# Attention's P V in a fused attention and mixture-of-experts kernel: fp32 operands in one product for three products of fp16 halves

## The chip, the cores and the metric

One Trainium2 chip (trn2), one of its cores. The metric is device time in microseconds of one execution of the whole kernel, taken as the median of several runs. The engines are named as in the profile: PE (TensorE matmuls), PEld (TensorE weight loads), DVE (VectorE), ACT (ScalarE), POOL (GpSimd), SP (the queue that issues most DMAs).

## What is computed

Attention over keys and values that are averaged in groups of 8, then a mixture-of-experts layer in which each token goes to its best expert. Batch 8, 8 heads, 576 tokens, head size 64; 72 pooled keys per head; 8 experts.

```python
k_p = k.reshape(B, H, Sp, pool, D).mean(axis=3)      # 576 -> 72 rows
v_p = v.reshape(B, H, Sp, pool, D).mean(axis=3)
scores = scale * np.matmul(q, k_p.transpose(0, 1, 3, 2))
attn = np.exp(scores - np.max(scores, axis=-1, keepdims=True))
attn = attn / (np.sum(attn, axis=-1, keepdims=True) + 1e-09)
x = np.matmul(attn, v_p)                             # tokens x (8 heads * 64)
logits = x @ w_gate
expert_idx = np.argmax(logits, axis=1)
gate_w = softmax(logits)[best]
y = relu(x @ w1[expert_idx]) @ w2[expert_idx]
out = gate_w * y
```

## The kernel before

**Units.** The 4608 tokens are handled in 36 units of 128 tokens (`units`, L447 to L456). A batch has 576 tokens, so four whole units and a rest of 64; the rests of two batches share one unit (its `r` is None), so two batches make nine units. The loop over units (L1029) writes the instructions of all engines in their final order; there is no scheduler. In it, work of neighbouring units is interleaved: while unit i has its P V, the scores of units i+3 or so are formed.

**A unit's steps.** `g_qt` turns the queries on PE (L471) and ACT copies them out (L476). `g_s` forms scores: two matmuls of 128x144 in fp32 for each call (L498; L492 in a unit of two rests), two calls per unit. `g_min` takes the row minima of the negated scores on DVE (L508), `g_exp` the exponentials on ACT (L515), written as P to a buffer `both`. `u_pt` turns P on PE (five transposes, L522) into the PSUM tile `pp`, and ACT copies it to SBUF (L527). `u_pv` multiplies by V into the PSUM tile `po`. `u_nrm` divides by the row sums on DVE: L589, a reciprocal L591 and a product L593 that writes the token rows. There is one `pp` and one `po`, so a unit's transposes wait until the copies of the last one have been read, and its P V waits for the last one's L593.

**P V in halves.** The eight heads' 72 keys lie one after the other, cut in five chunks of 128 rows (`HS`, `SLOTS`), so a chunk holds pieces of two or three heads. V is laid out as `VB[b % 3]`: for each chunk and each of up to three heads (its slots) the 64 columns of V, 8 gate columns and a column of ones, 73 in all, set to zero in the rows of other heads by a mask. All of it is held twice in fp16: half 0 is V rounded, half 1 the rest. P too: L527 writes `ph` (fp16 of 256 P), and L533 on DVE forms the rest, `pl` (256 P minus ph). `u_pv` then takes three passes, ph with both halves of V, pl with the first one:

```python
for x, y in ((0, 0), (0, 1), (1, 0)):
    a = (ph, pl)[x]
```

Each pass has six matmuls, two each of 146, 219 and 73 columns, 18 for a unit (L559), 36 where two batches share the unit (L554, 64 output rows each).

**Preparing V of a batch** (`prep`, L837, and the hand-written hooks for batch 1). POOL sums groups of eight rows (`pool_k`, `pool_v`: L326, L328, L329). `v_pe` and `v_act` turn V; `v_high` writes its fp16 half on ACT (L397); `u_pe` multiplies V by the gate weights (L416, L418) into a PSUM tile `pu`; `v_copy` on ACT copies the high half into `pu` too (L410). On DVE, `v_dve` forms the low half (L402), `cross` scales the gate columns by the mask (L427), `both_halves` writes their two halves (L430, L431). Then `masked` writes V times the mask into `VB`, once per half (L441, 128x960), in two units running; in each of these units PE multiplies the mask by an identity (L525) so that it lies in `pp` beside P.

**Order between DVE's pieces.** Small steps of the routing (`route`: best expert, rank, positions of six units at a time) and the three steps of `u_dve` wait in a list, `fillers`; `fill()` takes one at fixed places of a unit (L1053, L1055, within `u_nrm`), and the steps of V are put at the list's head (L435).

**After attention.** Rows are scattered by expert in DRAM (L708, POOL), and from L1199 on the experts' products follow on PE: `up` (L1009 to L1018) and `finish` (L1097), in a loop over blocks of 256 tokens. The first products of block 0 stand already in units 33 to 35 (`UPAT`).

Of the kernel before, what the change touches and what calls it, by code (L numbers as in the profile page):

```python
# [17 lines left out]
POOL = 8  # L18
SX = 2.0 ** 6
SW = 2.0 ** 5  # L20
SV = 4.0
SP = 256.0
# [10 lines left out]
def kernel(  # L33
# [116 lines left out]
    mks = consts.tile([128, 5, 3], F32, name="mks")  # L150
    nc.vector.tensor_scalar(mks, mk, SV, None, op0=OP.mult)
    mk16 = consts.tile([128, 5, 3], F16, name="mk16")
    z16 = consts.tile([128, 5, 3], F16, name="z16")
    nc.vector.memset(z16, 0.0)
    nc.vector.tensor_copy(mk16, mk)
# [46 lines left out]
    for e in range(E):  # L202
# [10 lines left out]
    VB = [loads.tile([128, 2, 5, 3, CS], F16, name=f"vb{i}") for i in range(3)]  # L213
# [5 lines left out]
               for x in (VB[2].rearrange("p y c s x -> p (y c s x)").bitcast(F32),  # L219
# [163 lines left out]
    def v_act(b):  # L383
# [8 lines left out]
        if b:  # L392
            v_high(b)

    def v_high(b):
        vc = KVS["vc", b] = work.tile([128, 2, 5, D], F16, name="vc", bufs=2)
        nc.scalar.activation(vc[:, 0, :, 0:D], KVS["vp", b], AF.Copy, scale=SV)  # L397

    def v_dve(b):
        vp, vc = KVS.pop(("vp", b)), KVS["vc", b]  # L400
        hi = vc[:, 0, :, 0:D] if b == 0 else five(KVS["pu", b], UX, D)
        nc.vector.scalar_tensor_tensor(vc[:, 1, :, 0:D], vp, SV, hi, op0=OP.mult, op1=OP.subtract)  # L402
# [17 lines left out]
    def u_dve(b):  # L420
        pm = KVS["pu", b]
        ut = pm[:, 0:UX].rearrange("p (c s e) -> p c s e", s=3, e=E)
        gh, gl = (VB[b % 3][:, s, :, :, D:D + E] for s in range(2))
# [94 lines left out]
    def u_pt(i):  # L518
# [7 lines left out]
        ph = work.tile([128, 640], F16, name="ph")  # L526
        nc.scalar.activation(ph, pp[:, 0:640], AF.Copy, scale=SP)  # L527
        PP_[i] = (pp, ph)

    def u_lo(i):  # L530
        pp, ph = PP_[i]
        pl = work.tile([128, 640], F16, name="pl", bufs=1)
        nc.vector.scalar_tensor_tensor(pl, pp[:, 0:640], SP, ph, op0=OP.mult, op1=OP.subtract)  # L533
        PP_[i] = (ph, pl)

    def u_pv(i):
        b, r = units[i]
        ph, pl = PP_.pop(i)
# [3 lines left out]
        for x, y in ((0, 0), (0, 1), (1, 0)):  # L542
            a = (ph, pl)[x]
# [829 lines left out]
```

## Times and profile before

| | us |
|---|---|
| median of 3 runs | 610.09 (606.8 to 613.31) |
| the profiled execution | 607.39 |
| its span, first to last instruction | 604.4 |
| mean granted clock of TensorE over the span | 0.986 of full |

The profile is of one execution. "Busy" of PE is the union of its matmul records, each of which also holds the time in which its last results drain, so a busy PE may still have room. A matmul in fp32 shows as two records and two weight loads, a transpose in fp32 and a matmul in fp16 as one. Times in the timeline are starts and lengths from the span's start; what the next instruction on PE starts after is the time that an instruction takes of the engine.

### The profile page before, as it was taken

Reading aid. Unit: us, or ns where it says so; the run is one execution under the profiler, and the core shown is the slowest. Engines: PE = TensorE matmul, PEld = TensorE weight load, DVE = VectorE, ACT = ScalarE, POOL = GpSimd, SP = SyncE. Lnnn points to the kernel's source line nnn. Section 1 sums busy time; section 2 is a strip of 40 time slices with the busy share of each in tenths; the row PEclk is TensorE's granted clock in tenths of the full one; section 3 lists DMA queues with packets and bytes.
Section 4 is the critical chain, followed back from the end, with each engine's and each line's share of the span. In section 5 each row is a group of like instructions: output and inputs, shape, how many; then the busy total and the mean of one; then the engine's idle time right before and its main releaser. Section 6 shows DMA issues by size and latency. Waiting matters only on the chain.

```text
span 604.4 us, 15782 instructions
## 1 busy us (share of the span) xinstructions
PE 568.9 (94%) x4727; PEld 421.1 (70%) x4728; DVE 309.9 (51%) x616; ACT 291.5 (48%) x648; POOL 270.5 (45%) x529
## 2 busy tenths in 40 slices
PE   7888999998899989979999999999999999999994
PEld 7687879887786746747676765767756767657762
DVE  5768888997887173206743872324513551123122
ACT  2777789889952262217643662224422642122222
POOL 5698898998976632120441331131421142201221
PEclk9999999999999989989999999999999999999997
DMA  8999898885586839832986789233242323421200
GB/s 231 303 291 281 279 310 276 269 254 196 139 312 194 237 98 387 282 90 39 337 287 165 223 253 318 77 95 80 73 109 44 93 61 90 109 62 32 65 35 15
DMA packets 96274, 107.14 MB, mean 177 GB/s; under 512 B 54446, under 2 KB 64686, under 8 KB 96240
## 3 DMA queue, kind: packets, MB, share of 16 engines
q1 hardware_dynamic: 89520, 85.42, 49.9%
q0 software_dynamic: 6720, 21.28, 9.3%
q8 instruction: 19, 0.31, 0.2%
q14 instruction: 15, 0.12, 0.1%
HBM read 72.99 MB, written 23.37 MB: 159 GB/s over the span
## 4 chain that ended last, share of the span: by engine, by line
PE 74%; DVE 9%; ACT 8%; POOL 3%; issue 2%; DMA 2%; SPq 0%; ACTq 0%; POOLq 0%; PEld 0%; DVEq 0%
PE po L1097 17%; PE pq L1097 15%; PE ps L1018 8%; PE pp L1018 4%; PE pq L1018 4%; PE ps L1009 3%; PE ps L1010 3%; PE ps L1011 3%; PE po L559 2%; ACT both L515 2%; PE ps L498 2%; PE pp L522 2%; PE pp L1009 2%; PE pp L1011 2%; PE pp L1010 2%
## 5 line engine op out<-in xcount | busy, mean ns | idle before, releaser
L1097 PEld LDWEIGHTS <-bd 128*128 128x128 f16 x936 | 91.4, 98 | 105.5
L1091 DVE SCALAR_TENSOR_TENSOR bd<-ps,bd 128x512 f16<-128x512 f32 (+1 forms) x44 | 27.6, 630 | 183.7 <-ACT bd L1088 183.6
L1258 POOL TENSOR_TENSOR spacer<-ql,iG 1x1 f32<-1x1 f32 x44 | 20.3, 462 | 196.2 <-ACT ql L1254 193.9
L515 ACT ACTIVATE both<-ps,nmx 128x72 f32<-128x72 f32 x288 | 68.5, 331 | 11.3 <-DVE nmx L508 10.3
L1088 ACT ACTIVATE bd<-ps 128x512 f16<-128x512 f32 (+1 forms) x44 | 24.0, 549 | 97.6 <-PE L1018 75.6
L1097 PE MATMUL po<-w,bd 128*128 128x512 f16 x264 | 58.9, 379 | 0.0
L1097 PE MATMUL po<-kv,bd 128*128 128x512 f16 x264 | 58.8, 379 | 0.0
L1018 PEld LDWEIGHTS <-qt 128*128 128x128 f16 x528 | 49.4, 101 | 12.5 <-issue 5.1
L1259 POOL DMA_INDIRECT out_dram<-ql,iG x44 | 46.2, 1051 | 21.4 <-issue 20.3
L1018 PEld LDWEIGHTS <-w 128*128 128x128 f16 x480 | 42.2, 100 | 9.9 <-ACT kv L116 2.6
L498 PE MATMUL ps<-bd,qT 128*128 128x144 f32 x256 | 45.6, 302 | 2.9 <-ACT both L515 0.9
L1097 PE MATMUL pq<-kv,bd 128*128 128x512 f16 x216 | 48.1, 379 | 0.0
L1097 PE MATMUL pq<-w,bd 128*128 128x512 f16 x192 | 42.9, 379 | 0.0
L1254 ACT ACTIVATE ql<-po,gB 128x512 f32<-128x512 f32 x22 | 15.0, 683 | 57.0 <-PE L1018 35.0
L708 POOL DMA_INDIRECT x_by_expert<-both,rpos x36 | 35.5, 987 | 14.1 <-issue 5.5
L498 PEld LDWEIGHTS ps<-bd,qT 128*128 128x128 f32 x256 | 34.8, 190 | 4.6 <-ACT both L515 1.4
L1018 PE MATMUL ps<-kv,qt 128*128 128x256 f16 (+1 forms) x264 | 32.9, 269 | 4.4 <-issue 4.0
L918 DVE TENSOR_TENSOR bd<-vb,bd 128x1024 f16<-128x1024 f32 x22 | 27.0, 1226 | 17.3 <-issue 7.3
L1254 ACT ACTIVATE ql<-pq,gB 128x512 f32<-128x512 f32 x22 | 15.0, 681 | 42.7 <-PE pq L1097 41.0
L533 DVE SCALAR_TENSOR_TENSOR pl<-pp,ph 128x640 f16<-128x640 f32 x36 | 29.5, 821 | 11.7 <-ACT ph L527 11.5
L326 POOL TENSOR_TENSOR st<-kv 128x1280 f32<-128x1280 f32 x12 | 34.9, 2905 | 0.0
L559 PE MATMUL po<-vb,ph 128*128 128x146 f16 (+2 forms) x384 | 30.4, 227 | 3.6 <-ACT ph L527 2.5
(259 smaller groups left out, 1296.6 us busy)
## 6 DMA issues: line engine op xcount, KB each, us to landing
both<-in_moe_w_dram SPq DMA_DIRECT2D x6, 2048.0 KB, 11.6
st<-in_moe_w_dram SPq DMA_DIRECT2D x6, 2048.0 KB, 14.3
vb<-x_by_expert SPq DMA_DIRECT2D x16, 578.0 KB, 5.8
st<-in_moe_w_dram SPq DMA_DIRECT2D x8, 1024.0 KB, 7.6
kv<-in_k_dram SPq DMA_DIRECT2D x6, 1024.0 KB, 8.2
kv<-in_v_dram SPq DMA_DIRECT2D x6, 1024.0 KB, 10.6
qt<-in_q_dram SPq DMA_DIRECT2D x6, 1024.0 KB, 11.8
kv<-in_k_dram SPq DMA_DIRECT2D x4, 512.0 KB, 4.8
```

The source lines that it names most:

```text
L326: nc.gpsimd.tensor_tensor(t1, src[:, :, 0:4 * D], src[:, :, 4 * D:], op=OP.add)
L498: nc.tensor.matmul(ps[:, x * 2 * KP:(x + 1) * 2 * KP], t[:, h, :], BD[b % 3][:, :, h, :], start=True, stop=True)
L515: nc.scalar.activation(p[:, h * KP:(h + 1) * KP], ps[:, x * KP:(x + 1) * KP], AF.Exp, bias=nmx[:, x:x + 1], scale=-1.0)
L559: nc.tensor.matmul(po[:, half, cols], a[:, c * 128:(c + 1) * 128], VB[b % 3][:, y, c, sl, 0:CW], start=st, stop=False, skip_group_check=True)
L708: st = nc.gpsimd.indirect_dma_start(out=xs, out_offset=bass.IndirectOffsetOnAxis(ap=Z["pos"][:, u:u + 1], axis=0), in_=X[:, u, :], in_offs ...
L1009: nc.tensor.matmul(dst, wh, xT[:, d, 0:n], start=(d == 0), stop=False)
L1010: nc.tensor.matmul(dst, wh, xT[:, DC + d, 0:n], start=False, stop=False)
L1011: nc.tensor.matmul(dst, wl, xT[:, d, 0:n], start=False, stop=(d == DC - 1))
L1018: nc.tensor.matmul(dst, W1[s][z][:, d, c], xT[:, x, 0:n], start=(z == 0 and x == 0), stop=(z == 1 and d == DC - 1))
L1097: nc.tensor.matmul(y, hT[x][:, f, 128 * j:128 * j + 128], W2[s][z][:, f, :], start=(half == x == z == f == 0), stop=(half == z == 1 and f ...
L1254: nc.scalar.activation(ys[j], pY[j], AF.Copy, scale=gB[:, j:j + 1])
L1259: st = nc.gpsimd.indirect_dma_start(out=out, out_offset=bass.IndirectOffsetOnAxis(ap=iG[:, j:j + 1], axis=0), in_=ys[j], in_offset=None, b ...
```

## The change

P and V stay in fp32. `u_pt` copies P once, unscaled, as fp32 (`pt`); `u_lo` and with it the low half of P are gone. `VB` has one fp32 copy in place of two fp16 ones, of the same size in bytes. `masked` runs once per batch and reads the pooled V itself, so `v_high`, `v_copy` and `v_dve` are gone. The gate columns are written by one product with the mask. `u_pv` has one pass of six matmuls in fp32. The scales of P and V (256 and 4) leave `u_nrm`. The mask is put beside P in one unit per batch where it was two.

```diff
-    VB = [loads.tile([128, 2, 5, 3, CS], F16, name=f"vb{i}") for i in range(3)]
+    VB = [loads.tile([128, 5, 3, CS], F32, name=f"vb{i}") for i in range(3)]
...
     def blank(i):
-        nc.gpsimd.memset(VB[i][:, 1, :, :, 72:73], 0.0)
-        nc.gpsimd.tensor_tensor(VB[i][:, 0, :, :, 72:73], mk16[:, :, :, None], z16[:, :, :, None], op=OP.add)
+        nc.gpsimd.tensor_tensor(VB[i][:, :, :, 72:73], mk[:, :, :, None], z15[:, :, :, None], op=OP.add)
...
-        if b:
-            v_high(b)
-
-    def v_high(b):
...
-    def v_dve(b):
...
-    def v_copy(b):
-        nc.scalar.activation(five(KVS["pu", b], UX, D), KVS["vc", b][:, 0, :, 0:D], AF.Copy)
...
         def cross():
-            KVS.pop(("pu", b))
-            nc.vector.tensor_tensor(ut, ut, mks[:, :, :, None].to_broadcast([128, 5, 3, E]), op=OP.mult)
-
-        def both_halves():
-            nc.vector.tensor_scalar(gh, ut, 1.0, None, op0=OP.mult)
-            nc.vector.tensor_tensor(gl, ut, gh, op=OP.subtract)
-            KVS["whole", b] = True
-
-        first = [lambda: v_dve(b)] * (b > 0) + [cross, both_halves]
-        fillers[0:0] = [(-1, False, f) for f in first]
-
-    def masked(b, s):
-        assert b == 0 or KVS["whole", b]
-        vc = KVS["vc", b] if s == 0 else KVS.pop(("vc", b))
+            nc.vector.tensor_tensor(VB[b % 3][:, :, :, D:D + E], ut, mk[:, :, :, None].to_broadcast([128, 5, 3, E]),
+                                    op=OP.mult)
+
+        fillers[0:0] = [(-1, False, cross)]
+
+    def masked(b):
         m = five(KVS["pp"], MK, 3) if b else KVS["m0"]
-        nc.vector.tensor_tensor(VB[b % 3][:, s, :, :, 0:D], vc[:, s, :, None, :].to_broadcast([128, 5, 3, D]),
+        nc.vector.tensor_tensor(VB[b % 3][:, :, :, 0:D], KVS.pop(("vp", b))[:, :, None, :].to_broadcast([128, 5, 3, D]),
                                 m[:, :, :, None].to_broadcast([128, 5, 3, D]), op=OP.mult)
...
-        ph = work.tile([128, 640], F16, name="ph")
-        nc.scalar.activation(ph, pp[:, 0:640], AF.Copy, scale=SP)
-        PP_[i] = (pp, ph)
-
-    def u_lo(i):
-        pp, ph = PP_[i]
-        pl = work.tile([128, 640], F16, name="pl", bufs=1)
-        nc.vector.scalar_tensor_tensor(pl, pp[:, 0:640], SP, ph, op0=OP.mult, op1=OP.subtract)
-        PP_[i] = (ph, pl)
+        pt = PP_[i] = work.tile([128, 640], F32, name="pt")
+        nc.scalar.activation(pt, pp[:, 0:640], AF.Copy)
...
-        for x, y in ((0, 0), (0, 1), (1, 0)):
...
+        for c in range(5):
+            h0, hend = HS[c] + SLOTS[c][0], HS[c] + SLOTS[c][1]
...
+                for s in range(2 if r is None else 1):
+                    m = slice(0, 128) if r is not None else slice(64 * s, 64 * s + 64)
+                    nc.tensor.matmul(po[m, half, cols], pt[:, c * 128 + m.start:c * 128 + m.stop],
+                                     VB[(b + s) % 3][:, c, sl, 0:CW], start=first.get(half, True), stop=False,
+                                     skip_group_check=True)
...
-    def put_masked(b, *at):
-        for s, i in enumerate(at):
-            mask_at.add(i)
-            put(i, "dve", masked, b, s)
+    def put_masked(b, at):
+        mask_at.add(at)
+        put(at, "dve", masked, b)
...
-        put(u[0], "act", v_copy, b)
...
-        u_lo(i)
```

On PE, between the scores of a unit and its P V, before the change (`ps` scores, `pq` turned queries and values, `po` the P V; one pass of three is shown):

```order
L498 MATMUL ps<-bd_159,qT 128x144 x2
L471 MATMUL pq<-ident,qt_154 128x128 x4
L375 MATMUL pq<-ident,vp 128x128 x2
L377 MATMUL pq<-ident,vp 64x128
L379 MATMUL pq<-ident,kp 64x64
L559 LDWEIGHTS ph
L559 MATMUL po<-vb_161,ph 128x146
L559 LDWEIGHTS ph
L559 MATMUL po<-vb_161,ph 128x219
L559 LDWEIGHTS ph
L559 MATMUL po<-vb_161,ph 128x73
```

And at the same step of a batch in the changed kernel, with the whole of its P V and what follows (a matmul in fp32 loads its weights itself and has one row):

```order
L467 MATMUL ps<-bd_154,qT 128x144 x2
L440 MATMUL pq<-ident,qt_151 128x128 x4
L368 MATMUL pq<-ident,vp 128x128 x2
L370 MATMUL pq<-ident,vp 64x128
L372 MATMUL pq<-ident,kp 64x64
L513 MATMUL po<-vb_159,pt 128x146
L513 MATMUL po<-vb_159,pt 128x219
L513 MATMUL po<-vb_159,pt 128x73
L513 MATMUL po<-vb_159,pt 128x146
L513 MATMUL po<-vb_159,pt 128x219
L513 MATMUL po<-vb_159,pt 128x73
L467 MATMUL ps<-bd_154,qT 128x144 x2
```

What stands ahead of P V is the same; the 18 matmuls on two tiles have become six on one.

On DVE, where the routing of six units meets the gate columns of a batch, before the change (`vc`, `vb` and `pq` of V and its gate columns, `ra`, `rm`, `roh` of the routing, `pl` the low half of P, `ri` and `both` of the division):

```order
L640 TENSOR_TENSOR pq<-pq,rm 128x48
L402 SCALAR_TENSOR_TENSOR vc<-vp,pq 128x320
L427 TENSOR_TENSOR pq<-pq,mks 128x120
L430 TENSOR_SCALAR vb_163<-pq 128x15x8
L431 TENSOR_TENSOR vb_163<-pq,vb_163 128x15x8
L589 TENSOR_SCALAR ri<-po 128x8
L646 TENSOR_TENSOR pq<-pq,down 128x48
L647 TENSOR_REDUCE rm_1937<-pq 128x6
L591 RECIPROCAL ri<-ri 128x8
L657 TENSOR_TENSOR roh<-pq,rm_1937 128x48
L593 TENSOR_TENSOR both<-po,ri 128x576
```

The same place in the changed kernel, up to the next unit's division:

```order
L595 TENSOR_TENSOR pq<-pq,rm 128x48
L403 TENSOR_TENSOR vb_159<-pq,mk 128x15x8
L544 TENSOR_SCALAR ri<-po 128x8
L601 TENSOR_TENSOR pq<-pq,down 128x48
L602 TENSOR_REDUCE rm_1596<-pq 128x6
L546 RECIPROCAL ri<-ri 128x8
L612 TENSOR_TENSOR roh<-pq,rm_1596 128x48
L548 TENSOR_TENSOR both<-po,ri 128x576
L477 TENSOR_REDUCE nmx<-ps 128x4 x2
L671 TENSOR_REDUCE rso<-roh 128x8
L544 TENSOR_SCALAR ri<-po 128x8
```

Four steps that read the tile of the gate columns have become one, and between the two minima of a unit there is no `pl`.

## Rows read from the trace of the kernel before

**Rows 1.** Busy us (and instructions) of each engine in four stretches of attention

```profile
core 0: us, PE busy (x) PEld busy (x) DVE busy (x) ACT busy (x) POOL busy (x), PEclk, DMA share, GB/s
39.34:58.09 18.75, 16.62 (x167) 14.44 (x167) 15.62 (x40) 14.13 (x48) 18.27 (x12) 1.00 1.07 290
58.09:122.88 64.79, 61.26 (x665) 55.91 (x663) 56.55 (x143) 56.36 (x184) 57.33 (x70) 1.00 0.89 284
122.88:163.22 40.34, 35.28 (x379) 31.70 (x378) 33.19 (x88) 36.76 (x109) 35.40 (x48) 1.00 0.61 196
163.22:180.87 17.65, 16.00 (x206) 13.83 (x205) 14.52 (x44) 11.02 (x31) 14.11 (x28) 1.00 0.87 280
```

**Rows 2.** The same for L533 alone, once per unit, in two stretches

```profile
58.09:122.88 64.79, 12.34 (x15) 1.00 0.89 284
122.88:163.22 40.34, 7.38 (x9) 1.00 0.61 196
```

**Rows 3.** Chain that ended last, by line: 58.09 to 122.88, then 122.88 to 163.22

```profile
by line: PE po L559 15.3%; PE ps L498 12.6%; PE pp L522 10.2%; ACT both L515 7.7%; ACT ph L527 5.5%; PE pq L471 5.0%; DVE pl L533 4.8%; DVE both L593 4.6%; ACT qT L476 3.9%; DVE vb L441 3.3%; issue 2.8%; DVE nmx L508 2.8%; DVE pq L633 2.7%;
...
by line: ACT both L515 15.4%; ACT ph L527 10.0%; DVE pl L533 9.9%; DVE nmx L508 8.4%; DVE vb L441 7.9%; DVE both L593 7.4%; PE pp L522 5.6%; issue 5.0%; ACT st L120 5.0%; ACT w L116 4.7%; DVE pq L633 3.9%; ACT qT L476 3.6%; DVE vb L431 1.5%
```

**Rows 4.** PE in order of time within one unit (start, length, idle before in brackets)

```profile
68.37 0.95 PE L559 MATMUL po<-vb,ph 128*128 128x146 f16 x12
69.15 0.55 PE L559 MATMUL po<-vb,pl 128*128 128x146 f16 x6
69.54 0.73 PE L498 MATMUL ps<-bd,qT 128*128 128x144 f32 x4
70.11 0.71 PE L522 MATMUL pp<-ident,both 128*128 128x128 f32 x5
70.65 0.29 PE L525 MATMUL pp<-mk,ident 128*128 128x15 f32 x2
70.80 0.74 PE L498 MATMUL ps<-bd,qT 128*128 128x144 f32 x4
```

**Rows 5.** PE in order of time near the start: fp32 matmuls of 144, 48 and 24 columns

```profile
20.35 1.15 PE L498 MATMUL ps<-bd,qT 128*128 128x144 f32 x8
21.33 0.54 PE L416 MATMUL pq<-wgb,vT 128*128 128x48 f32 x4
21.80 0.40 PE L418 MATMUL pq<-wgl,vT 64*128 64x24 f32 x2
```

**Rows 6.** Instructions of removed or changed lines: count, ns min/median/max, first and last start

```profile
L533 DVE SCALAR_TENSOR_TENSOR pl<-pp,ph x36: 802/824/826, 24.6 to 178.5; 128x640 f16<-128x640 f32 x36
...
L441 DVE TENSOR_TENSOR vb<-vc,pp x14: 1132/1144/1155, 42.0 to 157.2; 128x960 f16<-128x960 f16 x14
...
L402 DVE SCALAR_TENSOR_TENSOR vc<-vp,pq x7: 477/487/489, 38.6 to 148.7; 128x320 f16<-128x320 f32 x7
...
L410 ACT ACTIVATE pq<-vc x7: 457/459/460, 38.1 to 148.1; 128x320 f32<-128x320 f16 x7
...
L397 ACT ACTIVATE vc<-vp x8: 460/476/527, 19.6 to 140.0; 128x320 f16<-128x320 f32 x8
```

**Rows 7.** PE's waits from 39.34 to 180.87: us in total, times, longest

```profile
PE po L559 <- ACT ph L527: 2.5, 4, 0.8
...
PE pq L738 <- DVE vb L431: 1.4, 1, 1.4
PE po L559 <- DVE pl L533: 1.4, 5, 0.6
```

**Rows 8.** Chain that ended last, 10 to 62 us, two of its pieces

```profile
33.21 2.87 POOL st L326
...
48.32 5.21 DMA bd<-bd
```

**Rows 9.** Chain that ended last, from 176 us on, two of its pieces

```profile
178.82 1.28 PE po L554 x36
...
187.40 2.59 PE pq L1097 x12
```

More of the change, by code (lines that the diff above doesn't have):

```diff
@@ L149 @@
     nc.vector.scalar_tensor_tensor(mk, rows, float(KP), mge, op0=OP.is_lt, op1=OP.mult)
[L150 to L155, printed above, removed]
+    z15 = consts.tile([128, 5, 3], F32, name="z15")
+    nc.gpsimd.memset(z15, 0.0)
     down = consts.tile([128, E], F32, name="down")
@@ L218 @@
     xg, xg2 = (x[:, 0:2 * XW].rearrange("p (j x) -> p j x", j=2)
-               for x in (VB[2].rearrange("p y c s x -> p (y c s x)").bitcast(F32),
+               for x in (VB[2].rearrange("p c s x -> p (c s x)"),
                          qt[0].rearrange("p h r d -> p (h r d)")))
@@ L391, in v_act @@
         nc.scalar.activation(vT[0:64, 256:384], pm[0:64, 256:384], AF.Copy)
-        if b:
-            v_high(b)
-    def v_high(b):
-        vc = KVS["vc", b] = work.tile([128, 2, 5, D], F16, name="vc", bufs=2)
-        nc.scalar.activation(vc[:, 0, :, 0:D], KVS["vp", b], AF.Copy, scale=SV)
-    def v_dve(b):
-        vp, vc = KVS.pop(("vp", b)), KVS["vc", b]
-        hi = vc[:, 0, :, 0:D] if b == 0 else five(KVS["pu", b], UX, D)
-        nc.vector.scalar_tensor_tensor(vc[:, 1, :, 0:D], vp, SV, hi, op0=OP.mult, op1=OP.subtract)
     UX = 120
@@ L420, in u_dve @@
     def u_dve(b):
[L421 to L423 removed]
+        ut = KVS.pop(("pu", b))[:, 0:UX].rearrange("p (c s e) -> p c s e", s=3, e=E)
         def cross():
[L426 to L439 removed]
+            nc.vector.tensor_tensor(VB[b % 3][:, :, :, D:D + E], ut, mk[:, :, :, None].to_broadcast([128, 5, 3, E]),
+                                    op=OP.mult)
+        fillers[0:0] = [(-1, False, cross)]
+    def masked(b):
         m = five(KVS["pp"], MK, 3) if b else KVS["m0"]
[L441 removed]
+        nc.vector.tensor_tensor(VB[b % 3][:, :, :, 0:D], KVS.pop(("vp", b))[:, :, None, :].to_broadcast([128, 5, 3, D]),
                                 m[:, :, :, None].to_broadcast([128, 5, 3, D]), op=OP.mult)
@@ L541, in u_pv @@
         first = {}
-        for x, y in ((0, 0), (0, 1), (1, 0)):
-            a = (ph, pl)[x]
-            for c in range(5):
-                h0, hend = HS[c] + SLOTS[c][0], HS[c] + SLOTS[c][1]
-                while h0 < hend:
-                    half = h0 // 4
-                    h1 = min(hend, 4 * half + 4)
-                    sl = slice(h0 - HS[c], h1 - HS[c])
-                    cols = slice((h0 - 4 * half) * CW, (h1 - 4 * half) * CW)
-                    st = first.get(half, True)
-                    if r is None:
-                        for s in range(2):
-                            nc.tensor.matmul(po[64 * s:64 * s + 64, half, cols],
-                                             a[:, c * 128 + 64 * s:c * 128 + 64 * s + 64],
-                                             VB[(b + s) % 3][:, y, c, sl, 0:CW], start=st, stop=False,
-                                             skip_group_check=True)
-                    else:
-                        nc.tensor.matmul(po[:, half, cols], a[:, c * 128:(c + 1) * 128],
-                                         VB[b % 3][:, y, c, sl, 0:CW], start=st, stop=False, skip_group_check=True)
-                    first[half] = False
-                    h0 = h1
+        for c in range(5):
+            h0, hend = HS[c] + SLOTS[c][0], HS[c] + SLOTS[c][1]
+            while h0 < hend:
+                half = h0 // 4
+                h1 = min(hend, 4 * half + 4)
+                sl = slice(h0 - HS[c], h1 - HS[c])
+                cols = slice((h0 - 4 * half) * CW, (h1 - 4 * half) * CW)
+                for s in range(2 if r is None else 1):
[3 more added lines that the diff above has]
+                                     skip_group_check=True)
+                first[half] = False
+                h0 = h1
     GRP = {}
@@ L588, in u_nrm @@
         ri = work.tile([128, 2, 4, 1], F32, name="ri")
-        nc.vector.tensor_scalar(ri, pv[:, :, :, 72:73], 1e-9 * SP, POOL * SV / SX, op0=OP.add, op1=OP.mult)
+        nc.vector.tensor_scalar(ri, pv[:, :, :, 72:73], 1e-9, POOL / SX, op0=OP.add, op1=OP.mult)
         fill()
@@ L801 @@
     turned_q()
-    v_high(0)
     u_pt(0)
     v_pe(0)
-    masked(0, 0)
-    v_dve(0)
+    masked(0)
     v_act(0)
@@ L813 @@
     drain(0)
-    masked(0, 1)
     g_min(1, 1)
@@ L842, in prep @@
         put(u[0], "pe" + u[1], u_pe, b)
[L843 removed]
         put(u[0], "dve", u_dve, b)
[L845 to L846 removed]
+        put_masked(b, u[0] + {2: 2, 4: 3, 5: 2}.get(b, 1))
     put(0, "act2", k_pe, 1)
@@ L852 @@
     put(2, "pe", u_pe, 1)
-    put(2, "act", v_copy, 1)
     put(2, "dve", u_dve, 1)
     put_masked(1, 3)
-    mask_at.add(4)
-    put(4, "pe", masked, 1, 1)
     put(1, "sp", load_kv, 3, kf)
```

6 lines of the change are left out of this document (1 added, 5 removed).

## The prediction, made before the changed kernel had run

> **What bounds the kernel now.** I read the busy time by stretches first. From 39.34 us on I cut attention into four stretches at starts of the division's product; they hold 4, 15, 9 and 5 of the 36 units (the 15 and the 9 in [rows 2]). The reader is to see in [rows 1] that no engine stands out: in the second stretch PE is busy 61.26 of 64.79 us (95%) with DVE, ACT and POOL at 87 to 88%; in the third ACT has 36.76 of 40.34 (91%) and PE 87%. The granted clock is 1.00 throughout, which is the 2.4 GHz level, so no stretch loses to the clock. The chain that ended last says the same by line [rows 3]: in the second stretch its largest pieces are PE's (P V, scores, transposes), in the third the exponentials and the copy of P on ACT, with DVE between them. Ahead of 58 us the chain goes through POOL's sums of keys and values and through a DMA that copies a block of keys [rows 8]. At its end it is PE's again: the P V of the last unit, then the experts' first products [rows 9]. What attention gains or loses therefore moves the end one for one: behind 187 us lie the experts' products, and the change touches nothing in them.
>
> **PE: the cost of the new P V.** A unit's 18 fp16 matmuls begin at 68.37 and the scores behind them at 69.54 [rows 4]: 1.17 us. Those scores are four records and take 0.57 us to 70.11. In a long run the same records need less: eight of them take 20.35 to 21.33, 0.1225 us each [rows 5], so four need 0.49. The 0.08 between is a weight load that the last short fp16 matmul doesn't cover. P V costs PE 1.25 us with it.
>
> The new P V has six fp32 matmuls, two each of 146, 219 and 73 columns, each of two records. At 0.1225 us for 144 columns, or 0.85 ns a column, a record of 146 takes 0.124, of 219 0.186, of 73 0.062. For the short ones the rows say more: four records of 48 columns take 21.33 to 21.80, 0.1175 each [rows 5], where the columns alone would be 0.041. A weight load sets that pace, and 73 columns lie nearer to 48 than to 144. I take 0.1175: 4 x (0.124 + 0.186 + 0.1175) = 1.71 us, so +0.46 per unit. The lower end is 0.062 for the short ones, 1.49 and +0.24; the upper leaves the 0.08 in place, +0.54. A unit of two rests runs its halves beside each other on PE's columns; I give it the same.
>
> The trace tells what a column costs, and the sum rests on that. The Trainium skill (FP8 and Floating Point Precision, TensorE Precision Notes) says that true fp32 takes four passes through the array: four where there were three, a rule that speaks against this change. The rows agree as to rate: two records at 0.85 ns a column are 1.7 ns, four times one fp16 column at 2.4 GHz. But by the rule alone P V would be 1.17 x 4/3 = 1.56, +0.31 a unit, and the sum below would end at -0.7 us in place of +2.3, as it doesn't hold the short matmuls' weight loads.
>
> The mask's matmul is needed once per batch, not twice: seven go, at 0.15 us each (70.65 to 70.80 [rows 4]), some 1.1 us, of which I put 0.7 into the second stretch.
>
> **DVE: what goes.** 36 low halves of P at 0.824 us are 29.7 us; eight of 16 masked copies at 1.144 are 9.2; the low half of V, seven times 0.487, is 3.4; two short steps per batch go too [rows 6]. That is over 42 us, about 1.2 per unit. The masked copy that stays reads fp32: not below the 1.144 it has, and by the 1.29 ns an element of L533 up to 1.24; it runs eight times on an engine that is now far from full, so I cost it nothing, and at worst 0.8 us if nothing hid it. What this buys is only what PE or ACT waited for DVE: P V for `pl` 1.4 us, a small matmul of the routing 1.4 for the gate columns' tile [rows 7]. Late next are the copy of P on ACT, for which P V waited 2.5 us, and PE itself.
>
> **ACT.** The two copies of V go, 8 x 0.476 and 7 x 0.459 [rows 6], 0.93 us per batch. The copy of P writes fp32 in place of fp16. In the same rows a copy of 320 elements to fp32 takes 0.459 and one to fp16 0.476, so I cost that at nothing; 36 times 0.02 either way is 0.7 us.
>
> **What moves.** No step changes its place in the list of units. The steps of V take one place of the fillers and not three, so the routing's small steps on DVE come up to two places earlier. No DMA, none of SP's queue and no scatter changes its unit; POOL's only change is among its first few us. No wait is added: `masked` waits for the mask in `pp` as it did, and P V of a batch's first unit for `masked`. The pooled V is held until `masked` has read it; its buffer's next writer is two batches on.
>
> **The sum, by stretches.** Up to 39 us POOL sums one batch after another whatever PE does, with a piece of 2.87 us at its end [rows 8]; the extra P V of three units lies beside it: 0. In the first stretch 4 x 0.46 = 1.8 us meet 2.1 us in which PE was idle, and that idle time was POOL's and the DMA's of 5.21 us, which end when they end: +0.2. In the second, 15 x 0.46 - 0.7 = +6.2 us of PE meet 3.5 us of idle; I let all of it be filled, since DVE's waits go and the longer P V gives ACT time: +2.7. In the third, 9 x 0.46 = 4.1 us of PE fit into 5.1 of idle, ACT stays the pace, and two batches' copies leave it: -1.9. In the fourth, 5 x 0.46 = 2.3 meet 1.65 of idle, of which I let 1.0 be filled: +1.3. Together **+2.3 us**: 609.7 for the profiled execution (607.39, its span of 604.4 and 3.0 around it), and by the median of the runs, 610.09, **612.4**. The three runs spread from 606.8 to 613.31, so about 1%, 6.1 us, is what can be told from no change.
>
> **Rivals.** (a) *PE's waits do not shrink* (slower). In each unit PE turns P, ACT copies it, and P V waits for the copy; in that loop P V comes after the wait, so a longer P V need not shorten it. If every idle time of PE stays, all is added: 33 x 0.46 - 1.1 = +14.1, 624. It decides from the point where PE, unit by unit, still stands idle before P V as long as now. For it: the copy of P was the longest wait of P V [rows 7] and 10% of the chain in the third stretch [rows 3]. Against it: 2.5 us of that wait in 141 is little, and ACT gets 0.46 us more per unit to be ready.
>
> (b) *DVE was the hidden pace, and short fp32 matmuls cost their columns* (faster). With +0.24 per unit the second stretch has 3.6 - 0.7 - 3.5 = -0.6, the fourth 1.2 - 1.65 = -0.4; and if the third falls from ACT's pace to PE's own 35.28 + 2.2 = 37.5, it gives -2.9. Sum -3.9, 606. To pass 1% ACT's and POOL's part of the other stretches would have to shrink too, and both are at 87% or more. For it: low halves and masked copies on DVE alone are 9.9% and 7.9% of the third stretch's chain [rows 3]. Against it: the 48-column records.
>
> (c) *The relief in the third stretch is absent* (ACT's other work closes up behind the copies, or the weights' splitting sets the pace): +4.2, 614. Still within 1%.
>
> **Chances.** The forecast with (c) and the milder half of (b) 0.67, (a) wholly or by more than half 0.24, faster than 604 0.09. So faster by over 1% 0.09, within 1% 0.67, slower 0.24. The range goes from 604, a little past (b), to 622, just short of (a) in full; the forecast's own is 608 to 617.
>
> **What would show it.** Right: one P V takes PE 1.65 to 1.75 us; the records of 73 columns start 0.11 to 0.12 us apart; PE is busy 97% or more in the second stretch, and DVE, without 12.34 us of low halves [rows 2] and some 7 us of V's steps, falls below 60% of it; the 15 units there take 66 to 69 us, the nine behind them 38 to 40; the loop of the experts is as long as it was. Wrong: PE still under 95% there with P V waiting for the copy of P (then (a)), short records at 0.06 (then (b)), or a difference that arises behind 190 us.

## The result, and the profile after

| | before | changed |
|---|---|---|
| median, us (20 runs each) | 610.57 (606.8 to 615.48) | 604.61 (603.42 to 608.92) |
| ratio, 95% interval | | 0.9906 (0.988 to 0.9931) |
| profiled execution, its span | 607.39, 604.4 | 608.13, 606.2 |

The kernel became faster by 0.94%, 6.0 us; +2.3 had been forecast. That lies within the 1% called "no change" ahead, but outside the interval of the measurement, and on the other side. Medians take in every run, ratios leave out a run that is over 1.5% above the fastest of its kernel, so a ratio can differ from that of the medians. The profiled execution of the changed kernel is one of its longest: ScalarE stood still for 9.8 us at the start of the experts' part, which none of the other profiles of it repeats. So attention is read from it, and the whole from the lists of runs.

The four stretches of [rows 1], cut at the same units (4, 15, 9, 5 of them), in the changed kernel:

```profile
38.18:57.00 18.82, 18.36 (x149) 17.09 (x147) 10.63 (x30) 13.21 (x46) 18.35 (x12) 1.00 1.10 286
57.00:121.95 64.95, 64.95 (x549) 61.88 (x548) 38.54 (x113) 53.28 (x177) 58.19 (x72) 1.00 0.87 283
121.95:160.12 38.17, 37.19 (x313) 35.34 (x311) 23.46 (x70) 35.26 (x106) 32.72 (x44) 1.00 0.58 199
160.12:179.18 19.06, 18.85 (x177) 17.07 (x176) 10.87 (x39) 11.14 (x31) 16.11 (x31) 1.00 0.89 279
```

TensorE (the first engine) now fills the second stretch to 100%, with DVE at 59%. Still the stretch is only 0.16 us longer than in [rows 1], and the third 2.17 us shorter. One P V, in order of time on PE as in [rows 4]:

```profile
71.94 1.81 PE L513 MATMUL po<-vb,pt 128*128 128x146 f32 x12
73.58 0.70 PE L467 MATMUL ps<-bd,qT 128*128 128x144 f32 x4
```

It takes 1.64 us up to the scores, where the 18 fp16 matmuls took 1.17 (1.25 with the 0.08 by which the scores behind them were longer) and 1.71 was forecast. Over the 36 units it is 1.64 or 1.65 us in 13, 1.72 to 1.75 in 21 and 1.84 in two. The starts of its two records of 73 columns and of the record behind them, from three cuts of the same view:

```profile
72.56 0.51 PE L513 MATMUL po<-vb,pt 128*128 128x73 f32 x3
72.63 0.45 PE L513 MATMUL po<-vb,pt 128*128 128x73 f32 x2
72.74 0.46 PE L513 MATMUL po<-vb,pt 128*128 128x146 f32 x2
```

The second record of 73 starts 0.06 us behind the first, the next matmul 0.11 behind that; the forecast had 0.1175 for each. The record of 146 that follows then takes 0.173 us, where the other three take 0.125 to 0.13.

PE's waits from 38.18 to 179.18 (the view lists these two), which answer to [rows 7], and the changed DVE and ACT operations (ns min/median/max), which answer to [rows 6]:

```profile
PE po L513 <- ACT pt L496: 1.2, 3, 0.7
PE ps L467 <- DVE nmx L477: 0.5, 1, 0.5
```

```profile
L410 DVE TENSOR_TENSOR vb<-vp,pp x7: 1130/1144/1150, 39.9 to 149.8; 128x960 f32<-128x960 f32 x7
L403 DVE TENSOR_TENSOR vb<-pq,mk x6: 273/273/273, 51.4 to 147.1; 128x120 f32<-128x120 f32 x6
...
L496 ACT ACTIVATE pt<-pp x33: 684/705/772, 39.0 to 175.7; 128x640 f32<-128x640 f32 x33
```

The masked copy from fp32 costs the 1.144 us that the fp16 one did, and the fp32 copy of P 0.705, where the fp16 copy took 0.704. No wait for the gate columns' or the low halves' operations is left.

### The profile page after: what moved, and what is told of

Read it like the earlier page. It is cut to its first block, busy times and chain, and to the rows that moved or that the text cites. A ratio compares the mean times of both kernels' runs of the same rounds, so it can differ in the third digit from the quotient of the medians.

```text
span 606.2 us, 15226 instructions
## 1 busy us (share of the span) xinstructions
PE 581.4 (96%) x4473; PEld 436.6 (72%) x4474; DVE 268.2 (44%) x545; ACT 285.0 (47%) x633; POOL 270.7 (45%) x527
## 4 chain that ended last, share of the span: by engine, by line
PE 51%; PEld 4%; issue 3%; ACT 1%; PEldq 0%; POOLq 0%; ACTq 0%; DVE 0%; POOL 0%; DVEq 0%
PE po L1042 14%; PE pq L1042 11%; PE ps L964 6%; PE pp L964 3%; PE pq L964 3%; PE ps L955 2%; PE ps L956 2%; PE ps L957 2%; PEld L964 1%; PEld L1042 1%; PE pp L957 1%; PE pq L956 1%; PE pq L957 1%; PE pp L955 1%; PE pq L955 1%
## 5 line engine op out<-in xcount | busy, mean ns | idle before, releaser
L513 PE MATMUL po<-vb,pt 128*128 128x146 f32 (+5 forms) x480 | 66.8, 301 | 1.2 <-ACT pt L496 1.2
L513 PEld LDWEIGHTS po<-vb,pt 128*128 128x128 f32 (+1 forms) x480 | 62.1, 178 | 4.4 <-ACT pt L496 2.5
L1042 PE MATMUL pq<-w,bd 128*128 128x512 f16 x192 | 44.7, 389 | 1.6 <-ACT bd L1033 1.6
L477 DVE TENSOR_REDUCE nmx<-ps 128x4 f32<-128x288 f32 x72 | 32.0, 452 | 11.1 <-PE ps L467 10.3
L496 ACT ACTIVATE pt<-pp 128x640 f32<-128x640 f32 x36 | 25.5, 709 | 23.3 <-PE pp L491 14.3
```

What stands on the lines that cost most here:

```text
L477: nc.vector.tensor_reduce(nmx, ps[:, 0:4 * KP].rearrange("p (h x) -> p h x", x=KP), axis=AX.X, op=OP.min)
L496: nc.scalar.activation(pt, pp[:, 0:640], AF.Copy)
L513: nc.tensor.matmul(po[m, half, cols], pt[:, c * 128 + m.start:c * 128 + m.stop], VB[(b + s) % 3][:, c, sl, 0:CW], start=first.get(half, Tr ...
L1042: nc.tensor.matmul(y, hT[x][:, f, 128 * j:128 * j + 128], W2[s][z][:, f, :], start=(half == x == z == f == 0), stop=(half == z == 1 and f ...
```

## The experiments

Theory A: the time was won in attention, where VectorE had kept TensorE waiting. Theory B: VectorE was hidden. Theory C: much of it was won outside attention, where the kernels wait for their own code. Each comparison has its own runs of the kernel before beside it. The expectations of e11 to e18 cut the stretches one unit later than [rows 1]: by that cut the second and third took 65.3 and 38.7 us before, 64.6 and 37.8 in the changed kernel, 65.1 and 38.6 in e2. The rows and the text here keep the cut of [rows 1].

**What the fp32 P V costs TensorE.** Both kernels run each product of scores of the whole units twice, so that TensorE sets the pace in both:

```diff
-                nc.tensor.matmul(ps[:, x * 2 * KP:(x + 1) * 2 * KP], t[:, h, :], ...)
+                for _ in range(2):
+                    nc.tensor.matmul(ps[:, x * 2 * KP:(x + 1) * 2 * KP], t[:, h, :], ...)
```

e7_fp16_no_low_scores2: 

> The kernel of e1_fp16_no_low (fp16 P V, no low half on VectorE; the low half of P is left out of the result) with each product of scores of the whole units run twice, 0.98 us more per unit on TensorE, so that TensorE is the pace of the second stretch in it and in the next one alike. Its second stretch minus that of the next gives what the fp32 P V costs TensorE. By the prediction's rows TensorE needs 64.57 - 6.2 = 58.4 in the second stretch without the doubling, so 58.4 + 14 = 72 to 73.5 us with it.

e8_fp32_scores2: 

> The changed kernel with the same doubled scores: second stretch 64.57 + 14 = 78.5 to 80 us. Between it and e7_fp16_no_low_scores2: 6.2 us if the prediction's +0.46 per unit holds (less 0.7 for the mask's matmuls), 9 if the stretch of 64.57 hid a dearer P V, 4 or less if the fp16 P V was cheaper to replace than its rows said.

Second and third stretches, first of e7 (fp16), then of e8 (fp32), columns as in [rows 1]:

```profile
60.21:132.89 72.68, 72.63 (x773) 69.46 (x772) 46.70 (x127) 56.07 (x184) 59.89 (x71) 1.00 0.79 248
132.89:173.46 40.57, 40.57 (x439) 39.21 (x439) 27.09 (x79) 36.17 (x108) 31.92 (x45) 1.00 0.55 186
```

```profile
61.31:139.79 78.48, 78.48 (x661) 75.57 (x660) 39.48 (x113) 53.35 (x177) 59.95 (x71) 1.00 0.72 230
139.79:184.35 44.56, 44.56 (x376) 43.12 (x375) 23.88 (x70) 35.79 (x106) 33.34 (x50) 1.00 0.51 169
```

PE is full in all four, and in none does the profile show a wait of PE for another engine, so the differences are PE's own price: 5.80 and 3.99 us, where the prediction had 15 x 0.46 - 0.7 = 6.2 and 9 x 0.46 = 4.1. The price was right. Subtracted from the 64.95 of the changed kernel it leaves 59.15 us that the fp16 kernel needs of PE in the second stretch. That stretch took 64.37 to 64.79 us in the four profiles of before's attention, so PE had 5.2 to 5.6 us to spare there.

**Is PE the pace now?** The first product of P V three times (e3):

```diff
-                    nc.tensor.matmul(po[m, half, cols], pt[...], ...)
+                    for _ in range(3 if c == 0 else 1):
+                        nc.tensor.matmul(po[m, half, cols], pt[...], ...)
```

> The changed kernel with the first matmul of P V (146 columns) run three times, so four records of 0.124 us more per unit, 0.50 us on TensorE. If TensorE is now the pace of attention from its second stretch on: 15 x 0.5 in the second, 5 x 0.5 in the fourth, and 4 to 4.5 in the third, together +14 to +15, 619 us. If there is room left in each unit (the waits for the copy of P): under +8, 612 us.

Measured: 621.31 us, ratio 1.0297 (1.0245 to 1.035). The second and the third stretch:

```profile
58.60:131.69 73.09, 73.09 (x617) 70.18 (x616) 38.78 (x114) 53.41 (x176) 59.62 (x71) 1.00 0.76 246
131.69:173.79 42.10, 41.93 (x352) 40.23 (x351) 23.55 (x70) 35.81 (x106) 32.81 (x45) 1.00 0.53 179
```

The second grew by 8.14 us, 0.54 per unit, and all of it shows: no room is left. The third grew by 3.93 us, where 9 x 0.54 = 4.9 were put on PE, so there PE had some 1 us of room.

**Where PE's idle time had come from: the low halves of P.** e1 takes the high half again in the third pass, so DVE is rid of L533 and PE works as before. e2 puts such an operation back into the changed kernel.

```diff
-        PP_[i] = (pp, ph)
+        PP_[i] = (ph, ph)
...
-        u_lo(i)
```

```diff
+        nc.vector.scalar_tensor_tensor(pl, pp[:, 0:640], 256.0, pt, op0=OP.mult, op1=OP.subtract)
```

e1_fp16_no_low: 

> The kernel before, its third pass of P V read from the high half again: TensorE has the same 18 fp16 matmuls per unit, VectorE is rid of 36 low halves (29.7 us). The low half of P is left out of the result. Theory A (TensorE's idle time in attention was VectorE's doing, and the change won because it went): TensorE's idle time vanishes without the dearer P V, so attention ends 5 to 8 us sooner than before, some 604 us. Theory B (the time is won behind attention, VectorE was hidden): within 1.5 us of before, 610.

e2_fp32_dve: 

> The changed kernel with one operation per unit put back on VectorE, in the low half's old place and of its size (640 elements from PSUM and from the copy of P, some 0.82 us), whose result nobody reads. Theory A: attention is 3 to 5 us longer than in the changed kernel, 608 to 610 us. Theory B: VectorE has room, the time stays at 605 within 1 us.

Second and third stretches, e1 and then e2:

```profile
56.72:120.25 63.53, 60.19 (x665) 55.87 (x663) 46.10 (x128) 55.62 (x184) 56.62 (x69) 1.00 0.92 290
120.25:157.21 36.96, 33.38 (x369) 30.73 (x370) 26.80 (x78) 35.42 (x109) 32.99 (x44) 1.00 0.62 207
```

```profile
57.90:122.53 64.63, 64.63 (x546) 61.56 (x545) 49.63 (x128) 53.70 (x176) 58.02 (x71) 1.00 0.87 274
122.53:162.18 39.65, 38.13 (x317) 35.91 (x315) 29.91 (x79) 35.86 (x106) 33.70 (x45) 1.00 0.59 197
```

Without the low halves the fp16 kernel gains 0.8 to 1.3 us in the second stretch and 3.38 in the third. In the changed kernel they cost the third stretch 1.48 us and the second nothing. Yet e1 as a whole was no faster (602.56, ratio 0.9998, 0.9963 to 1.0033), nor e2 (603.60, 1.0004, 0.9965 to 1.0043). e1 gave its gain back in attention's last units, where ACT waited for the rows of the experts' next block:

```profile
ACT bd L909 <- DMA vb<-x_by_expert: 4.1, 1, 4.1
```

That load is late next once attention is quicker. In the changed kernel it was waited for in two of six profiles (e4, e10).

e13 was to tell VectorE's load from the longer hold of P's tile in PSUM, with `zf.to_broadcast([128, 640])` in the place of `pt`:

> As e2_fp32_dve, but the operation put back on VectorE reads P's tile in PSUM and a constant, so that it runs beside the copy of P on ScalarE and not behind it: the same load on VectorE (0.82 us per unit), P's tile held no longer than the copy holds it. If VectorE's load alone makes the second and third stretches of e2 (65.1 and 38.6 us): the same again. If the longer hold of P's tile does: 64.6 and 37.8, as in the changed kernel.

The stretches were e2's (64.62 and 39.65), but the operation did not do what it was made for: in every unit it began 0.03 us or more behind the end of ACT's copy, as in e2. The Trainium skill (PSUM — Partial Sum Buffer, Terms) says that two engines must not be on one bank of PSUM at once, reads included; that would be the reason, and the rows agree in that no unit has the two side by side. The traces settle the question all the same: in the second and third stretches of e2 and e13 the operation ended 1.4 us or more before the next unit's first transpose into P's tile (at 64.38, against 65.82 us, in one unit of e2). No unit there waited for the tile, so what is left is VectorE's load.

e12 was to do the same with the operation on SBUF alone (`pt` for `pp[:, 0:640]`):

> As e2_fp32_dve, but the operation put back on VectorE reads the copy of P in SBUF alone and no longer P's tile in PSUM, so the tile is free as early as in the changed kernel. If VectorE's load was what cost e2 its 0.55 and 0.8 us in the second and third stretches: 65.1 and 38.6 us again. If it was that P's tile in PSUM was held longer (it has one buffer, and the next unit's turns wait for it): 64.6 and 37.8, as in the changed kernel.

It took 621.2 us, and tells nothing on the question: its operation became another one (last section).

**The steps of V.** e17 makes the gate columns in one operation in the kernel before (their low half is left out), e18 leaves out the low half of V too, e16 makes the masked copy twice in the changed kernel.

```diff
-            nc.vector.tensor_tensor(ut, ut, mks[...].to_broadcast([128, 5, 3, E]), op=OP.mult)
-        def both_halves():
-            nc.vector.tensor_scalar(gh, ut, 1.0, None, op0=OP.mult)
-            nc.vector.tensor_tensor(gl, ut, gh, op=OP.subtract)
-        first = [lambda: v_dve(b)] * (b > 0) + [cross, both_halves]
+            nc.vector.tensor_tensor(gh, ut, mks[...].to_broadcast([128, 5, 3, E]), op=OP.mult)
+        first = [lambda: v_dve(b)] * (b > 0) + [cross]
```

```diff
+        for dst in (VB[b % 3][:, :, :, 0:D], vb2):
+            nc.vector.tensor_tensor(dst, KVS["vp", b][...], m[...], op=OP.mult)
```

e17_fp16_gate1: 

> The kernel before with the gate columns in one operation on VectorE per batch in place of three (their low half is left out: zero), the low half of V on VectorE and all else as before. In the second stretch only units 12 and 18 of attention, which hold the routing's products, were 1.1 and 1.4 us longer before (6.1 and 6.6 us) than in the changed kernel (5.0 and 5.2), whether the low halves of P run on VectorE or not. If the gate columns' three steps in the fillers did that (TensorE waits for their tile): units 12 and 18 fall by 0.5 to 1 us each, the second stretch to 63.5 to 64.5 us. If the low half of V ahead of them in the same queue did it: no change here, all of it in e18_fp16_gate1_v1. If neither: both stay as before.

e18_fp16_gate1_v1: 

> As e17_fp16_gate1, and the low half of V goes too, on VectorE (0.49 us per batch) and its copy on ScalarE (0.46); both masked copies stay, the second made from the high half (so the low halves of V and of the gate columns are left out). If V's steps were what TensorE waited for at units 12 and 18: both fall to 5.2 us or less, the second stretch to 62.5 to 63.5 us with the low halves of P still on VectorE, more than the 1.7 us that their absence gave in e1_fp16_no_low.

e16_after_mask2: 

> The changed kernel with the masked copy of V made twice per batch (the second into a tile nobody reads), 1.14 us more on VectorE per batch. If VectorE has room wherever TensorE is the pace: second stretch 64.6 as before, third within 0.3 of 37.8, so the V part of the change is worth nothing by itself. If it is on the path at the batches' turns: 0.5 us or more in the second stretch.

Second and third stretches of e17, then of e16:

```profile
55.25:117.45 62.20, 60.74 (x659) 55.26 (x657) 54.45 (x137) 55.94 (x184) 57.67 (x69) 1.00 0.92 295
117.45:156.20 38.75, 35.17 (x381) 31.88 (x379) 32.07 (x84) 36.59 (x109) 35.15 (x48) 1.00 0.65 199
```

```profile
57.44:122.40 64.96, 64.96 (x549) 61.89 (x548) 42.65 (x117) 53.28 (x177) 58.12 (x72) 1.00 0.87 282
122.40:161.39 38.99, 37.49 (x313) 35.35 (x311) 25.45 (x72) 35.26 (x106) 32.69 (x44) 1.00 0.58 198
```

Two short operations less per batch (e17) make the second stretch 2.2 to 2.6 us shorter and the third 1.6, more in the second than 15 low halves of 0.82 us did. By the cut of the expectations the second took 62.4 us, less than the 63.5 to 64.5 said. Units 12 and 18, from one reciprocal's start to the next, fell by 0.76 us each (6.10 to 5.34, 6.55 to 5.79). The waits say part of why; PE's over attention in the kernel before (run e15, stretches 1 to 4):

```profile
PE pq L738 <- DVE vb L431: 1.4, 1, 1.4
...
PE pq L471 <- DVE vb L431: 0.8, 1, 0.8
...
PE pq L727 <- DVE vb L431: 0.7, 1, 0.7
```

In e17 none of these is there. Only the 0.8, in unit 18, lies in the second stretch; the other two lie in the third. Transposes of queries and the routing's products share two PSUM tiles with the gate columns, and the columns' last step (L431) lies three places deep in the fillers. The edit also gives one place of the fillers back to the routing's steps; the runs don't tell that from the shorter work. e18 gains 0.8 more in the second stretch (61.37) and 0.1 in the third; units 12 and 18 fell to 4.94 and 5.49 us, the second of them not to the 5.2 expected. The second masked copy costs the changed kernel 0.82 us over both stretches, nearly all of it at one unit.

**Attention alone.** Both kernels end behind the loop over units (the experts are left out):

```diff
     assert not hooks
+    nc.sync.dma_start(out[0:128, :], XR[:, 0, 0:Dm])
+    return
```

e9_before_attention: 

> The kernel before, ended behind its 36 units of attention (with their routing, scatters and early loads); the experts are left out, so the result is not computed. Some 190 us. To be set beside e10_after_attention: what the change does to attention, without the experts' one-off waits. Theory A (won in attention): before is longer by 4 to 6 us. Theory C (a smaller part in attention, the rest behind it): by 1 to 2.5 us.

e10_after_attention: 

> The changed kernel ended at the same place. Theory A: 4 to 6 us shorter than e9_before_attention; theory C: 1 to 2.5 us shorter.

Medians of five runs: 187.22 (186.23 to 188.56) and 186.35 (186.04 to 187.12), so -0.9 us, with ranges that overlap. Theory A's 4 to 6 us are excluded. By the start of the last unit's division product (178.72 us in e15, 178.37 in e14) attention is 0.35 us shorter, so what it gained is small, 0.35 to 0.9 us, and not clear of noise.

**How far the whole wanders.** The changed kernel again, twice, and the kernel before against itself:

e11_after_again: 

> The changed kernel as it is, on the chip of these runs, beside the kernel before. If its 0.9906 of the first comparison holds: 0.988 to 0.993. Attention from the seventh unit on is the same to 0.1 us (second stretch 64.6, third 37.8); what differs from run to run lies ahead of 61 us and between 183 and 280 us.

e14_after_third: 

> The changed kernel as it is, a third time, on whatever chip this is. If only attention's 0.9 us and some 0.5 us ahead of and behind the span are the change's, and the rest of the first comparison was chance behind attention: ratio 0.994 to 1.000. If the first 0.9906 holds on every chip: 0.988 to 0.993.

e15_before_null: 

> The kernel before against itself: how far such a ratio wanders by chance alone. If the one-off waits behind attention fall evenly over runs: 1.000 within 0.002. If they come in streaks (per load of a program, or per chip): up to 0.005 off.

| run | median, us | of before beside it | ratio |
|---|---|---|---|
| e11 | 601.12 | 602.50 | 0.9969 (0.9935 to 1.0003) |
| e14 | 601.36 | 604.24 | 0.9936 (0.9897 to 0.9974) |
| e15 | 603.36 | 604.24 | 0.9986 (0.9946 to 1.0026) |

The gain is 2 to 4 us in these two (1.4 and 2.9 by the medians), so beside attention's part there seems to be something else, and the null run's interval shows that a ratio can be some 0.4% off by chance. Part of e14's gain goes with the clock: over the runs of its ratio the mean granted clock was 0.994, against 0.991 in the kernel before; in e11 both had 0.9935. A straight line through the lists of e11, e14 and e15 (0.66 us per 0.001 of clock, my estimate) leaves 2.0 us between the kernels at a like clock, with a standard error of 0.35. Whether the change itself moves the clock is not shown.

**Something else: the end.** Behind the last matmul both kernels do the same, but the span ends 8.76 and 8.82 us after it in the two profiles of the kernel before, and 7.10 to 7.11 after it in the changed one (four profiles, with e4's). In e15 and e14 the last matmuls end within 0.04 us of each other, at 589.05 and 589.08. DMA queues from 594 us to the span's end in e15 (the same view of e14 has no packet), and DVE's last drains (first and last start), e15 and then e14:

```profile
q14 instruction: 1, 0.01, 0.8%
```

```profile
L1368 DVEq DRAIN  x2: 10/14/18, 594.7 to 597.6; - x2
```

```profile
L1313 DVEq DRAIN  x2: 10/10/10, 594.7 to 595.7; - x2
```

DVE, for which all others wait there, goes on 1.9 us late, after a piece of 8 KB of instructions has been fetched. The changed kernel's shorter DVE program has no such fetch. A second piece is fetched 0.3 us behind the span in before, and what an execution takes beyond its span was 2.3 to 2.7 us (medians of five lists of it) against 1.95 to 2.06 in four of the changed kernel; but e3 has 2.7, so that half microsecond is not tied to the change. Together 1.7 + 0.5 = 2.2 us, and with attention 2.6 to 3.1: between the two repeats' 1.9 and 3.9 (ratios times 604).

The other runs bear out that the last fetch goes with the length of an engine's program and not with fp32. In e1, e7, e17 and e18, the kernel before with 16 to 29 fewer DVE instructions in the trace, the span ends 7.09 to 7.11 us behind the last matmul and DVE is not late. In e6, the changed kernel with some 200 more on SP, it is SP whose last step comes 2 us behind the others', after a piece of 8 KB, and the span ends 9.04 us after the last matmul; in e5, the kernel before with the same edit, it ends 7.38 us after it. DVE's drains in e1, then SP's waits in e6:

```profile
L1361 DVEq DRAIN  x2: 10/10/10, 596.6 to 597.6; - x2
```

```profile
L1316 SPq EVENT_SEMAPHORE  x14: 17/28/28, 598.8 to 602.3; - x14
```

**The experts' loop.** Theory C had looked for it in TensorE's branches. The branch to the code of one weight slot, at its first pass near 262 us, in the kernel before, in e1 and in e5 (ns min/median/max):

```profile
L1318 PEldq COMPARE_BRANCH  x3: 189/375/5605, 260.6 to 262.7; - x3
```

```profile
L1311 PEldq COMPARE_BRANCH  x3: 189/373/2990, 258.7 to 260.8; - x3
```

```profile
L1319 PEldq COMPARE_BRANCH  x3: 189/363/3305, 259.6 to 261.8; - x3
```

In e4 the warming matmuls were fewer (`WARM = 64`). In e5 and e6 five tiny transfers stand ahead of the turning one (the "late turn"):

```diff
         with tc.If(more[0] > 0):
+            for x in range(5):
+                nc.sync.dma_start(idle[:, 2 * x:2 * x + 2], w_gate[0:1, 0:2])
             trans()
```

e4_warm64: 

> The changed kernel with 64 warming matmuls at its start in place of 80: sixteen instructions fewer ahead of everything on TensorE, which stands idle there anyway. Theory C (the experts' part has waits at the first pass through each of its branches, whose length hangs on where the instructions lie and when they are fetched, not on P V): attention as in the changed kernel, and the part behind 187 us longer or shorter by 2 us or more. If that part hangs on nothing of the kind: 605 within 1 us.

e5_before_late_turn: 

> The kernel before; in the experts' loop SyncE issues five tiny transfers ahead of the transfer that turns the next block, so that one starts some 2.5 us later. Attention is untouched. Theory C (the part behind 190 us has one-off waits of TensorE's branches for their code, and the code comes late where the 256-byte pieces of that turning transfer are under way, 5.6 us in the profile of before against 3.0 to 3.4 where the branch came first): the branch near 263 us falls to 3.0 to 3.5 us, TensorE's stall there from 4.2 to under 2.5, and the median by 1.5 to 4 us against before. If the stall does not hang on that transfer: the branch keeps its 5 us or more and the time is that of before within 1 us, or longer by what the later turning costs.

e6_after_late_turn: 

> The changed kernel with the same five tiny transfers. Theory C: the branch near 265 us takes 3.0 to 3.5 us, and the time stays within 1 us of the changed kernel's or falls by up to 1.5; against the kernel before with the same edit only what attention gained is left, 1 to 2 us. If the change won its time in attention alone, the distance between the two stays at 6 us.

The branch fell to 3.3 us in e5 (3.45 in e6) as theory C had it, but both were slower than the kernel before beside them, 610.77 (1.0119, 1.0042 to 1.0197) and 607.14 (1.0061, 1.0023 to 1.0099): a new pause of TensorE of 2.1 us appeared near 310 us, and e5 took 4.7 us beyond its span, e6 1.4. So the 3.6 us between them, where 1 to 2 or 6 had been expected, are mostly, some 3 us, time beyond the span. e4 gave 600.10 (0.9938, 0.9893 to 0.9983), no other than the changed kernel without its edit. What the long branch is worth lies within chance: in e15 it took 3.36 us, so the kernel before does not have it always, and its experts' part, from the first product of `finish` to the last matmul (403.96 us), was then as long as the changed kernel's (403.69 in e11, 404.34 in e14). Nor is it the kernel before's alone. In 18 profiles with the loop the turning transfer's pieces of 256 bytes began ahead of the branch in five (before, the changed kernel's own, e3, e17, e18), by 0.1 to 0.8 us: the fetch of TensorE's code then began 1.9 to 3.2 us behind the branch's start, and the branch took 4.26 to 5.61. In the other 13 the pieces came later, the fetch began 0.6 to 1.0 us behind it, and the branch took 2.97 to 3.69. The loop was untouched, as forecast.

## Why the prediction was wrong

- **PE's price, right.** P V 1.64 to 1.75 us in 34 of 36 units where 1.65 to 1.75 was said; 5.80 us in the second stretch for 6.2, 3.99 in the third for 4.1. Its parts were less so, and that they cancel is luck: two matmuls of 73 columns cost 0.06 + 0.11 us each and not 2 x 0.1175, a record of 146 behind them some 0.05 more, and in most units the first record 0.1 more. The Trainium skill's rule (FP8 and Floating Point Precision, TensorE Precision Notes) of four passes in place of three gave 1.56; the trace, 1.64 and more, lies above it.
- **The step that failed:** "In the second, 15 x 0.46 - 0.7 = +6.2 us of PE meet 3.5 us of idle." All idle was filled, as assumed, but it was 5.2 to 5.6 us. The 3.5 were span minus busy, and a busy PE is not a full one: records reach past the time that the engine needs (59.15 needed, 60.88 to 61.26 busy). The stretch changed by +0.2 to +0.6, not +2.7: of the 2.1 to 2.5 us between, 1.7 to 2.1 are this idle time and 0.4 PE's price. That is nearly all the error of attention's sum. The Trainium skill (Perfetto Trace Analysis, Summary: the profiler window per engine type) says that the profiler's end of a TensorE operation is estimated; busy time that reaches 1.7 to 2.1 us past the need agrees with that.
- **DVE's share, wrongly placed.** "Two short steps per batch go too" was the dearest piece in the second stretch: without two of the gate columns' three steps the kernel before is 2.2 to 2.6 us shorter there (e17), without 15 low halves, 12.34 us of DVE, 0.8 to 1.3 (e1). In the third it is the other way round, 1.6 against 3.38. The 1.4 us of [rows 7] is one of three waits for the gate columns' last step, and it lies in the third stretch.
- **Third stretch, right in size and wrong in cause:** -2.17 for -1.9, which is luck. The prediction gave it to ACT's copies of V. Put back on DVE, the low halves cost it 1.48 (e2) and the second masked copy 0.82 (e16), 2.3 together, so little is left for the copies; no run took these away alone, and e18, without one of the two, gained 0.1. Nor did "ACT stays the pace" hold: PE is busy 37.19 of 38.17 us, its waits for the copy of P there come to 1.0, and of the 4.9 us that e3 added 3.93 showed.
- **Fourth stretch, right:** 17.65 to between 18.90 and 19.32 in four profiles, +1.25 to +1.67 for +1.3. Where the next block's rows came late it was 20.7 and 21.4. The first: 18.4 to 20.0 before, 18.1 to 18.8 after, for +0.2.
- **"A difference that arises behind 190 us" would be wrong,** it said, and there is one: 1.7 us with DVE's last fetch and perhaps 0.5 beyond the span. The change touches no instruction there; it moves the code.
- **Rivals.** (a) fell: PE's idle time was filled wholly. (b) had the side right, but by DVE's gate steps and not by short matmuls at their columns' price: its sign, short records 0.06 apart, came true within a matmul, but the twelve records and what follows them cost 1.64 and more, not 1.49. (c) fell.

What stays open: some 3 us of the first comparison's 6.0, which the repeats don't show. Both kernels were slower in it than in any later list (610.57 us against 602.50 to 604.78, and 604.61 against 601.12 and 601.36), and of its runs of the kernel before no granted clock is on record.

## What to carry to other kernels

Idle time of an engine is what it does not need, not what its busy share leaves: measure the need by making the engine the pace in both kernels and taking the difference. What an operation costs is not told by its length, and can differ from stretch to stretch: two small steps per batch at the head of a list, holding a PSUM tile, outweighed 15 operations of 0.82 us in one stretch (2.2 to 2.6 against 0.8 to 1.3 us) and were outweighed by nine of them in the next (1.6 against 3.38). From the runs a kernel of fp16 halves with the gate columns in one step looks quicker through attention's middle (100.95 us for two stretches against 103.12), but a form of it that keeps the low half was not tried.

## What the runs showed of the hardware

- **One operation, two sources.** On DVE `pl` from PSUM and SBUF (e2), and from SBUF alone (e12), with POOL's sum of 320 elements beside them:

```profile
L503 DVE SCALAR_TENSOR_TENSOR pl<-pp,pt x28: 802/825/826, 63.6 to 179.2; 128x640 f16<-128x640 f32 x28
```

```profile
L323 POOL TENSOR_TENSOR kp<-st x4: 864/866/868, 62.2 to 117.8; 128x320 f32<-128x320 f32 x4
```

```profile
L503 DVE SCALAR_TENSOR_TENSOR pl<-pt x25: 803/1041/3643, 61.5 to 178.4; 128x640 f16<-128x640 f32 x25
```

```profile
L323 POOL TENSOR_TENSOR kp<-st x4: 865/868/1329, 71.1 to 133.4; 128x320 f32<-128x320 f32 x4
```

  At best it is as quick (803 ns), but it can take 3.6 us, about one of POOL's sums of 1280 elements (2.9 us) more, and POOL's own operations stretch too; the kernel took 18.7 us more than before's 602.50 beside it, and 20.1 more than the changed kernel's 601.12 (e11). The Trainium skill (SBUF — State Buffer, SBUF: two separate sides) says that a DVE operation with two SBUF inputs and a GpSimd operation that reads SBUF lock each other out; these rows agree: in e12 an operation that met none of POOL's larger additions took 803 to 826 ns, and one that met a sum of 1280 elements ended behind it.
- **A fetch of code is late behind a transfer of small pieces.** One first pass of TensorE through a branch took 2.97 to 3.69 us in 13 profiles and 4.26 to 5.61 in the five in which 2048 pieces of 256 bytes began ahead of it (the loop's paragraph above).
- **The last instructions can cost a fetch:** 1.7 us at the end of the kernel before, gone with 16 fewer DVE instructions (e17).
- **Time goes with the granted clock from run to run.** In e14's list runs of 0.997 or more take 597.4 to 600.1 us and those of 0.990 take 602.9 and 603.9. The profiles show the 1.2 GHz level behind pauses of TensorE, but not behind each: with a pause of 1.1 to 1.3 us that ends between 31 and 34 us, the mean granted clock from 30 to 40 us was 0.66 in e1 and e12, 0.83 in e2, e4 and e18, and 1.00 in before, e15 and the changed kernel's profile.
